# Gate layer in seven half products from chunk 2 on, 64x64-tile attention from pair 12, one new written order

## The chip, the cores and the metric

The kernel runs on one core of one Trainium2 chip. A core has TensorE (PE, matrix products into PSUM), VectorE (DVE), ScalarE (ACT), GpSimd (POOL) and SyncE (SP, which here only issues transfers). The metric is the device time of one execution in microseconds, as the median of several runs.

## What is computed

Attention over 8 batches x 8 heads, 576 positions of 64 numbers each, and then a gated feed-forward layer over the 4608 tokens of 512 numbers. The attention of a head is the sum of two parts:

```python
q_d = q.reshape(B, H, Sd, factor, D).mean(axis=3)     # factor 4, also k_d, v_d
out_d = sm_attn(q_d, k_d, v_d)                        # softmax attention at 144 positions
out_up = np.repeat(out_d, factor, axis=2)
mask = np.abs(pos[:, None] - pos[None, :]) < factor   # each position sees 7
scores = scale * np.matmul(q, k.transpose(0, 1, 3, 2))
scores = np.where(mask, scores, -1000000000.0)
...                                                   # softmax, out_local = attn @ v
return (out_up + out_local).astype(np.float32)
```

```python
gate = np.maximum(x @ w_gate, 0.0)     # x: 4608 x 512, w_gate: 512 x 1536
val = x @ w_val
return (gate * val @ w_out).astype(np.float32)        # w_out: 1536 x 512
```

## The kernel before

**Units of work.** Attention goes by 32 pairs of heads, four pairs to a batch. The feed-forward layer goes by nine chunks of 512 tokens. A chunk needs all pairs of the batches that its tokens lie in; chunk 7 needs the last pairs. Matrices are f16 on the chip, sums f32 in PSUM, which has eight banks of 512 f32 columns.

**A pair.** q and k come by POOL's transfers (`emit_load_q1`), are transposed by a transfer that SP issues (`emit_qkT`) and pooled 4:1 by VectorE (`emit_pool`). `emit_s1_mm` (line 421) makes the local scores in 12 matmuls of 64 rows, 128 columns of weights and 96 moving columns, which cover 96 queries with 112 keys used, and the pooled scores in four of 144 columns. ScalarE takes the exponentials (`emit_exp`, two halves, and the pooled ones), VectorE multiplies the band mask in (`emit_mask`, two halves). From pair 8 on `emit_s2w_mm` (line 577) makes numerators and denominators in one: the weights of a matmul are 64 columns of v beside 64 columns of ones, so that half of the 128 output rows are sums and half denominators; the two heads differ in which half is which. So logarithm (`emit_ln`), and division by multiplying (`emit_xnw`, line 609), go by head on 64 rows of 720 columns. `emit_xsum` adds the local and the repeated pooled part into xT, the layer's input. Pooled v is summed by POOL (`emit_v2`, `emit_v1`) from a transfer of its own. Pairs 4 to 7 use another form, `emit_den` and `emit_num` on 64-column tiles.

**The feed-forward layer.** `emit_h_mm` (line 635) makes 128 of the 1536 hidden columns for 512 tokens with four matmuls of 512 columns, for the gate and for the value weights. ScalarE takes the gate's relu into r1, VectorE multiplies it with the values in PSUM into gT (`emit_gate`). The output product of every chunk goes by `Unit` (line 694): two units of 256 tokens a chunk, each a 2x2 block product done with seven half products (p1 to p7) of six 256-column matmuls in place of eight, on sums and differences of the blocks (`sums`, VectorE). Partial results are copied to SBUF by ScalarE (`keep`) and added to others by VectorE (c11, c12, c22) or copied by ScalarE (c21).

`Block` (line 887) does the same for the gate layer: two hidden groups j and j+6 for 512 tokens, seven products of two 256-column matmuls each (`q`, line 910), three `keep` copies, three VectorE sums and one copy, then relu and multiplication in one VectorE instruction (line 950). It is used for ten blocks: chunk 7 from j = 2 and all of chunk 8.

**The order.** It is written out by hand: every engine runs its instructions as emitted. FRONT holds loads, pairs 0 to 7 and chunk 0; ORDER is a period of one chunk with four pairs, repeated by `emit_periods`; TAIL holds the rest of the output layer and chunks 7 and 8. A token such as `hg/0/0` names a step, its argument and its half of the chunk. FRONT's 14 wide warm-up matmuls on zeros come first on TensorE; POOL's first own work is the load of pair 0's k.

Of the kernel before, what the change touches and what calls it, by code (L numbers as in the profile page):

```python
# [73 lines left out]
TAIL = """  # L74
p/1/60 wg/2/ hv/0/70 keep/1/60 hg/0/70 gate/5 gate/4 hv/1/70 relu/0/70 sumhi/0/60 next/0 hg/1/70
sumhi/1/60 next/1 xs/0/7 hg/1/71 relu/1/70 xs/1/7 wg/0/ p/2/60 qg/1/72 gate/0/70 qg/2/72
keepg/1/72 hg/0/71 relu/1/71 tg/11/72 gate/1/70 p/6/60 sum/2/60 hv/0/71 keep/2/60 wg/1/
relu/0/71 hv/1/71 xs/2/7 gate/0/71 qg/1/73 qg/6/72 p/7/60 c11//60 keepg/2/72 xs/3/7 keepg/1/73
qg/7/72 wg/3/ hv/0/72 keepg/3/72 keep/3/60 qg/6/73 qg/5/72 qg/4/72 tg/22/72 p/4/60 gate/1/71
qg/3/72 c21//60 p/5/60 sum/0/61 tg/21/72 tg/12/72 qg/2/73 hv/1/72 keepg/2/73 tg/11/73 sum/1/61  # L80
qg/7/73 gateg/0/72 p/1/61 keepg/3/73 c22//60 qg/5/73 qg/4/73 gateg/1/72 qg/1/74 tg/21/73 hv/0/73
tg/22/73 keepg/1/74 xs/0/8 keep/1/61 qg/2/74 sum/3/60 qg/1/75 qg/6/74 tg/11/74 qg/3/73 p/6/61
tg/12/73 keepg/2/74 qg/5/74 p/3/60 keepg/1/75 qg/2/75 c12//60 qg/7/74 hv/1/73 gateg/0/73
keepg/3/74 tg/11/75 qg/4/74 p/2/61 tg/22/74 tg/21/74 gateg/1/73 qg/6/75 qg/1/80 qg/3/74
keepg/1/80 hv/0/74 tg/12/74 keep/2/61 xs/1/8 keepg/2/75 qg/5/75 c11//61 qg/2/80 sum/3/61 qg/7/75
hv/1/74 keepg/3/75 tg/22/75 qg/4/75 sum/2/61 p/5/61 gateg/0/74 qg/6/80 qg/3/75 gateg/1/74 p/7/61
tg/12/75 hv/0/75 xs/2/8 keepg/2/80 xs/3/8 tg/21/75 qg/2/81 gateg/0/75 qg/7/80 hv/1/75 keepg/3/80
tg/11/80 keep/3/61 qg/1/81 p/4/61 keepg/1/81 tg/11/81 qg/4/80 c21//61 qg/5/80 c22//61 hv/0/80
tg/21/80 tg/22/80 gateg/1/75 qg/1/82 qg/3/80 keepg/1/82 qg/5/81 tg/12/80 hv/1/80 sum/0/70 p/1/70
gateg/1/80 qg/6/81 gateg/0/80 p/3/61 keepg/2/81 sum/2/70 qg/7/81 hv/0/81 keepg/3/81 sum/1/70  # L90
keep/1/70 c12//61 qg/2/82 tg/22/81 qg/4/81 hv/1/81 tg/11/82 qg/3/81 qg/6/82 tg/12/81 p/2/70
sum/3/70 keepg/2/82 p/6/70 tg/21/81 gateg/0/81 qg/7/82 sum/0/71 keep/2/70 qg/5/82 qg/2/83
keepg/3/82 p/7/70 tg/22/82 qg/4/82 keep/3/70 qg/1/83 qg/3/82 keepg/1/83 p/4/70 tg/12/82
gateg/1/81 hv/0/82 c21//70 c11//70 qg/6/83 tg/11/83 p/5/70 keepg/2/83 sum/2/71 tg/21/82 p/1/71
gateg/0/82 qg/7/83 c22//70 keep/1/71 qg/1/84 qg/2/84 keepg/3/83 qg/5/83 hv/0/83 keepg/1/84
tg/22/83 qg/3/83 qg/6/84 tg/12/83 qg/4/83 p/3/70 tg/11/84 tg/21/83 gateg/0/83 keepg/2/84 hv/1/82
sum/1/71 qg/7/84 gateg/1/82 qg/1/85 keepg/3/84 p/6/71 keepg/1/85 c12//70 qg/5/84 part/20/80
qg/2/85 tg/22/84 hv/1/83 part/00/80 sum/3/71 qg/3/84 qg/4/84 tg/12/84 hv/0/84 tg/21/84
gateg/1/83 p/2/71 tg/11/85 qg/6/85 c11//71 hv/1/84 keepg/2/85 gateg/0/84 keep/2/71 qg/5/85
gateg/1/84 qg/7/85 p/5/71 keepg/3/85 p/7/71 part/00/81 tg/22/85 qg/4/85 part/20/81 keep/3/71  # L100
hv/0/85 part/01/80 part/01/81 part/21/81 p/4/71 part/10/80 part/30/80 c22//71 qg/3/85 c21//71
hv/1/85 tg/12/85 tg/21/85 gateg/0/85 p/3/71 gateg/1/85 p/1/81 part/22/81 c12//71 p/1/80
part/21/80 part/11/80 part/31/80 p/2/80 keep/1/80 part/02/80 part/12/80 keep/1/81 p/2/81 c11//80
part/10/81 p/6/80 part/22/80 part/11/81 part/30/81 p/5/80 part/32/80 keep/2/80 part/02/81
part/12/81 p/7/80 p/6/81 keep/3/80 c22//80 p/4/80 keep/2/81 part/31/81 c11//81 p/7/81 c21//80
part/32/81 p/5/81 keep/3/81 p/3/80 c22//81 p/3/81 c12//80 p/4/81 c12//81 c21//81
"""
LATE = ("gate/5/1", "gate/4/1", "next/0/1", "next/1/1")
ORDER = """
p/1/0 gate/5/1< scores/a/0 keep/1/0 gate/4/1< hg/0/0 exp/a0/0 sumhi/0/0 sumhi/1/0 exp/a1/0  # L110
hv/0/0 mask/a0/0 ed/a/0 mask/a1/0 p/2/0 next/0/1< relu/0/0 next/1/1< o/a00/0 o/a01/0 c11//0
o/a10/0 ln/a0/0 o/a11/0 sum/2/0 p/6/0 v/a/1 sum/3/0 p/5/0 keep/2/0 pool/b/0 v2/b/0 ln/a1/0 p/7/0
hg/2/0 keep/3/0 after/3/0 v1/a/1 inv/a/0 c22//0 p/4/0 gate/0/0 v2/a/0 p/3/0 xn/a1/0 c21//0 relu/2/0 hg/1/0
xn/a0/0 qk/a0/1 hv/2/0 relu/1/0 qk/a1/1 c12//0 xsum/a/0 scores/b/0 qk/a2/1 next/0/0 hv/1/0
exp/b0/0 v/b/0 exp/b1/0 hg/4/0 mask/b0/0 gate/1/0 v4/a/1 ed/b/0 hg/3/0 mask/b1/0 relu/4/0
gate/2/0 v1/b/0 o/b00/0 o/b01/0 o/b10/0 pool/a/0 ln/b0/0 o/b11/0 hv/4/0 v2/a/1 ln/b1/0 hv/3/0
gate/4/0 inv/b/0 v4/b/1 next/1/0 p/1/1 relu/3/0 xn/b1/0 v4/b/0 p/2/1 keep/1/1 qk/a3/1 hg/5/0
xn/b0/0 qk/b0/1 p/6/1 gate/3/0 relu/5/0 qk/b1/1 scores/a/1 next/2/0 keep/2/1 next/3/0 hg/0/1
# [50 lines left out]
def kernel(  # L169
# [23 lines left out]
    NJJ = D_FF // 128  # L193
    LEAD = 4
    NTP = 9
    NVP = 11
    VS = 7
    NK = NJJ // 2
    B0 = 1
# [947 lines left out]
```

## Time and profile before

| | |
|---|---|
| median of 3 runs | 345.66 us (345.18 to 346.06) |
| profiled execution, span from first to last instruction | 343.5 us |
| mean granted TensorE clock | 0.998 |
| TensorE busy, matmuls | 335.8 us, 3244 |
| VectorE, ScalarE, POOL busy | 295.2, 218.3, 181.9 us |
| line 638, gate and value matmuls of 512 columns | 352 and 432 |
| line 650, gate multiplication, mean of one | 680 ns |
| line 757, `keep` copy of 128x256, mean of one | 373 ns |

The span leaves out what lies around the instructions, so the median stands a little above it. A busy share on the page counts time in which at least one instruction of the engine is under way; matmuls overlap, so the mean duration of one (379 ns for 512 columns) is longer than its distance to the next. Idle time of an engine stands with the instruction ahead of which it falls, and with what ended it.

### The profile page before, as it was taken

What the parts mean: (1) busy time and instruction counts of PE and PEld (TensorE: products, weight loads), DVE (VectorE), ACT (ScalarE), POOL (GpSimd) and SP (SyncE); (2) the same over time, 40 slices, a digit from 0 to 9 for tenths busy, and PEclk for the clock granted to TensorE, in tenths of its full rate; (3) what the DMA queues carried; (4) which work ended last, traced back from release to release, by engine and by line L of the source; (5) the groups of instructions that cost most, each with busy time, mean ns of one, the idle gap of its engine ahead of it and who ended that gap; (6) DMA issues with size and microseconds to landing.
All of it is one profiled execution on the core that took longest, in us unless ns stands there. A gap on an engine that the chain in (4) does not pass through costs nothing.

```text
span 343.5 us, 8292 instructions
## 1 busy us (share of the span) xinstructions
PE 335.8 (98%) x3244; PEld 216.0 (63%) x3244; DVE 295.2 (86%) x546; ACT 218.3 (64%) x423; POOL 181.9 (53%) x232
## 2 busy tenths in 40 slices
PE   7899999999999999999999999999999999999996
PEld 3765556756575756575666656665766557768785
DVE  6695679988999999999999999999999798886892
ACT  3878766767767776676667767776677633334222
POOL 8986547776999893969297878740300000000000
PEclk9999999999999999999999999999999999999999
DMA  9999999999999999999989996991100001001023
GB/s 133 165 170 187 186 191 160 148 163 159 213 139 176 148 183 87 132 133 163 125 100 147 145 161 80 158 150 37 47 17 32 31 2 46 32 31 61 28 67 108
DMA packets 167882, 39.87 MB, mean 116 GB/s; under 512 B 149820, under 2 KB 164772, under 8 KB 167844
## 3 DMA queue, kind: packets, MB, share of 16 engines
q0 software_dynamic: 132160, 22.63, 92.1%
q1 hardware_dynamic: 35572, 16.71, 27.0%
q8 instruction: 25, 0.41, 0.5%
q14 instruction: 13, 0.11, 0.1%
q10 hardware_dynamic: 112, 0.02, 0.0%
HBM read 45.72 MB, written 9.44 MB: 161 GB/s over the span
## 4 chain that ended last, share of the span: by engine, by line
PE 90%; ACT 4%; DVE 3%; DMA 2%; issue 1%; POOL 0%; DVEq 0%; ACTq 0%; POOLq 0%
PE ps L638 48%; PE ps L723 23%; PE ps L910 4%; PE ps L584 4%; PE ps L437 2%; PE ps L426 2%; PE ps L592 2%; DMA vw<-in_v_dram 1%; PE ps L363 1%; PE ps L407 1%; DVE ee L453 1%; ACT qkT L377 1%; ACT ee L447 1%; ACT ed L461 1%; DVE xn L611 1%
## 5 line engine op out<-in xcount | busy, mean ns | idle before, releaser
L638 PE MATMUL ps<-xT,wv_sb 128*128 128x512 f16 x432 | 109.0, 379 | 0.0
L638 PE MATMUL ps<-xT,wg_sb 128*128 128x512 f16 x352 | 88.4, 380 | 0.0
L647 ACT ACTIVATE r<-ps 128x512 f16<-128x512 f32 x88 | 52.0, 596 | 31.6 <-PE ps L638 28.5
L638 PEld LDWEIGHTS <-wv_sb 128*128 128x128 f16 x432 | 40.4, 98 | 39.7
L650 DVE TENSOR_TENSOR gT<-r,ps 128x512 f16<-128x512 f16 x88 | 59.0, 680 | 6.7 <-PE ps L638 3.9
L638 PEld LDWEIGHTS <-wg_sb 128*128 128x128 f16 x352 | 32.6, 98 | 32.3 <-issue 0.2
L611 DVE TENSOR_TENSOR xn<-ps,rden 64x720 f16<-64x720 f32 x48 | 43.4, 905 | 5.3 <-ACT rden L607 4.1
L602 ACT ACTIVATE rden<-ps 64x720 f32<-64x720 f32 x48 | 36.7, 765 | 14.4 <-PE ps L592 13.3
L447 ACT ACTIVATE ee<-ps 112x576 f16<-112x576 f32 x64 | 38.8, 648 | 5.9 <-PE ps L437 4.9
L308 POOL DMA_DIRECT2D qk<-in_k_dram x46 | 33.9, 740 | 8.4 <-DMA qk<-in_q_dram 3.8
L308 POOL DMA_DIRECT2D qk<-in_q_dram x46 | 33.8, 740 | 6.9 <-DMA qk<-in_k_dram 1.7
L453 DVE TENSOR_TENSOR ee<-ee,cst_sb 112x576 f16<-112x576 f16 x64 | 32.3, 524 | 5.8 <-ACT ee L447 5.2
L723 PEld LDWEIGHTS <-gT 128*128 128x128 f16 x324 | 31.5, 98 | 9.0
L723 PEld LDWEIGHTS <-xo 128*128 128x128 f16 x288 | 27.4, 98 | 7.4
L333 POOL DMA_DIRECT2D vw<-in_v_dram x30 | 28.8, 960 | 5.8 <-PE ps L638 1.5
L350 DVE TENSOR_REDUCE qkd<-qkT 128x288 f16<-128x1152 f16 x23 | 30.9, 1344 | 0.0
L757 ACT COPY q<-ps 128x256 f32<-128x256 f32 x45 | 16.8, 373 | 21.1 <-PE ps L723 20.7
L723 PE MATMUL ps<-wo_sb,gT 128*128 128x256 f16 x216 | 28.0, 273 | 0.0
L723 PE MATMUL ps<-wt,xo 128*128 128x256 f16 x216 | 27.7, 272 | 0.0
L385 POOL TENSOR_TENSOR v<-v 72x512 f32<-72x512 f16 x21 | 24.8, 1182 | 3.7 <-DMA v<-in_v_dram 3.1
L920 ACT COPY vw<-ps 128x256 f32<-128x256 f32 x30 | 10.8, 374 | 20.7 <-PE ps L910 13.8
L570 DVE TENSOR_TENSOR xT<-xn 128x576 f16<-128x576 f16 x28 | 22.6, 808 | 0.5
(110 smaller groups left out, 556.9 us busy)
## 6 DMA issues: line engine op xcount, KB each, us to landing
out_dram<-y_sb SPq DMA_DIRECT2D x24, 256.0 KB, 4.0
vw<-in_v_dram POOLq DMA_DIRECT2D x30, 168.0 KB, 6.8
qk<-in_q_dram POOLq DMA_DIRECT2D x46, 72.0 KB, 6.6
qk<-in_k_dram POOLq DMA_DIRECT2D x46, 72.0 KB, 6.6
v<-in_v_dram POOLq DMA_DIRECT2D x21, 144.0 KB, 6.9
out_dram<-y_sb SPq DMA_DIRECT2D x22, 128.0 KB, 1.7
wg_sb<-in_moe_w_gate_dram POOLq DMA_DIRECT2D x4, 384.0 KB, 9.7
wv_sb<-in_moe_w_val_dram POOLq DMA_DIRECT2D x4, 384.0 KB, 10.5
```

What stands on the lines that cost most here:

```text
L308: nc.gpsimd.dma_start(dst.rearrange("p (j h d) -> p j h d", h=2, d=64)[:, :, hh, :], _dap(src, off + hh * S * D, [[D, 96], [NQ * D, NB], [ ...
L333: nc.gpsimd.dma_start(t, _dap(v, base, [[D, WK], [NQ * D, n], [1, D]]))
L350: nc.vector.tensor_reduce(out=qkd[hp % 2].rearrange("p i t -> p (i t)"), in_=qkT[hp % 4][:, 0 : 2 * S].rearrange("p (t f) -> p t f", f=4), ...
L385: nc.gpsimd.tensor_tensor(out=m, in0=t[:, :, 0:128], in1=t[:, :, 128:256], op=ALU.add)
L447: nc.scalar.activation(out=o, in_=ps[0:WK, p0 + 2 * g : p0 + 2 * g + 2, 0:288], func=AF.Exp, scale=scale)
L453: nc.vector.tensor_tensor(out=o, in0=o, in1=_sap(masks_sb, (0, WK), 96 * g, [[0, 2], [1, 288]]), op=ALU.mult,)
L602: nc.scalar.activation(out=rden[lo : lo + 64], in_=ps[de : de + 64, 4 + 2 * hh : 6 + 2 * hh, 0:360], func=AF.Ln)
L611: nc.vector.tensor_tensor(out=xn[lo : lo + 64], in0=ps[lo : lo + 64, 4 + 2 * hh : 6 + 2 * hh, 0:360], in1=rden[lo : lo + 64], op=ALU.mult,)
L638: nc.tensor.matmul(out=out, lhsT=w[:, kk, bass.ts(jj, 128)], rhs=xT[:, kk, c * TCH : (c + 1) * TCH], start=(kk == 0), stop=(kk == 3),)
L647: nc.scalar.activation(out=r1[j % 3], in_=h1, func=AF.Relu)
L650: nc.vector.tensor_tensor(out=gT[c % 2][:, jj, :], in0=r1[j % 3], in1=h2, op=ALU.mult)
L723: nc.tensor.matmul(out=out, lhsT=left[:, i, :], rhs=right[i], start=(first and i == 0), stop=(i == NK - 1), skip_group_check=True,)
```

## The change

**Gate layer.** From chunk 2's fourth block on, every gate block goes by seven half products: 39 blocks in place of ten. What remains in the old form are chunks 0 and 1 and three blocks of chunk 2, which have relu on ScalarE as before. The sums of the weights (`emit_ws`) lie in the second halves of the vw buffers and, one of them, over the masks.

**Partial sums in PSUM.** A new class `Seven` serves the gate blocks and, from chunk 1 on, the output units. Where `Block` and `Unit` copied a partial result to SBUF three times and added it three times, ScalarE now copies it to where the next product is accumulated in PSUM (after product 1 into d, after product 2 into b), and one other product (5) to SBUF; two results are copied out by ScalarE (11, 21), two summed by VectorE (12, 22). Relu and gate are one VectorE instruction.

**Attention from pair 12.** All matmuls use 64 rows and 64 columns of TensorE; four in turn are of four different quarters. Queries go in groups of 48 with 64 keys, head h on its own half of the output rows. Exponential, mask, logarithm and division are one instruction a pair on 128 partitions. Scores use banks 4 and 5, denominators 4 and 5 again, numerators 6 and 7. v is loaded in two parts of 64 rows, its pooled part as f32 by two SP transfers in place of one of POOL, and the pooled result is copied to the other half of the partitions by two SP transfers (`emit_dup`). Three POOL memsets clear the v4 buffers at the start.

**Order.** ORDER and TAIL are replaced by one list, MAIN, that names pairs, chunks and blocks outright. FRONT is as before; MAIN begins with the scores of pair 12.

```diff
+MAIN = """
+s1/12 hg/2/0/0 hv/2/0/0 relu/2/0/0 ws/2/1 exp/12 lq/18/2 hg/2/1/0 flip/15 gate/5/1@1 hv/2/0/1 v2/14 gate/4/1@1
+pool/13 sum/1/0/0/5/6 gate/2/0/0 p/1/0/1 lq/20/2 lq/18/1 ed/12 relu/2/1/0 hg/2/0/1 hv/2/1/0 sum/1/0/2/0/6
...
+e/8/0/12 s/8/1/5 y/8/0/1/1 e/8/1/22 y/8/0/0/0 e/8/1/11 y/8/0/0/1 y/8/1/1/1 y/8/1/0/0 p/8/1/4 e/8/1/12 e/8/0/21
+y/8/1/0/1 y/8/0/1/0 e/8/1/21 y/8/1/1/0
+"""
...
+    ZP = 12
...
-    v4 = ring(NV4, [72, 4, 256], FP16, "v4_")
+    v4 = ring(NV4, [128, 3, 256], FP32, "v4_")
...
+    for t in v4:
+        nc.gpsimd.memset(t, 0.0)
...
+    def emit_load_v4z(hp, h):
+        b, off = head_off(hp)
+        nc.sync.dma_start(
+            v4[hp % NV4][64 * h : 64 * h + 48],
+            _dap(v, off + h * S * D, [[4 * D, 48], [192 * D, 3], [1, 4 * D]]),
+        )
...
+    def emit_dup(hp, n):
+        o = vdz[hp % 3]
+        nc.sync.dma_start(o[64 - 64 * n : 112 - 64 * n, 1], o[64 * n : 64 * n + 48, 0])
...
+    def emit_s1z(hp):
+        r4, f = hp % 4, qkdflat[hp % 2]
+        for c in range(3):
+            for g in range(2):
+                for h in range(2):
+                    rows, lo = slice(64 * h, 64 * h + 64), 288 + 72 * c
+                    nc.tensor.matmul(
+                        out=ps[64 * g : 64 * g + 64, 4 + h, lo : lo + 72].rearrange("p (j t) -> p j t", t=12),
+                        lhsT=f[rows, SD + 48 * c : SD + 48 * c + 64],
...
+        t = qkT[r4]
+        for j in range(6):
+            for par in range(2):
+                for h in range(2):
+                    rows, lo = slice(64 * h, 64 * h + 64), 96 * j + 48 * par
+                    nc.tensor.matmul(
+                        out=ps[64 * par : 64 * par + 64, 4 + h, 48 * j : 48 * j + 48],
+                        lhsT=t[rows, S + lo - 3 : S + lo + 61],
+                        rhs=t[rows, lo : lo + 48],
...
+    def emit_denz(hp):
+        for par in range(2):
+            rows = slice(64 * par, 64 * par + 64)
+            for h in range(2):
+                nc.tensor.matmul(
+                    out=ps[64 * h : 64 * h + 64, 4 + par, 0:288],
+                    lhsT=ones_sb[rows, 0:64],
+                    rhs=eefull[hp % 2][rows, h, 0:288],
...
+        emit_downz(hp, 4, lambda rows, other, c: ones_sb[rows, 64:128])
+
+    def emit_numz(hp):
+        t, d = vz[hp % NL], vdz[hp % 3]
+        for j in range(6):
+            for par in range(2):
+                rows = slice(64 * par, 64 * par + 64)
+                for h in range(2):
+                    nc.tensor.matmul(
+                        out=ps[64 * h : 64 * h + 64, 6 + par, 48 * j : 48 * j + 48],
+                        lhsT=t[rows, 6 * h + j, :],
+                        rhs=eefull[hp % 2][rows, h, 48 * j : 48 * j + 48],
...
+        emit_downz(hp, 6, lambda rows, other, c: d[rows, other, c, :])
...
-    class Block:
...
+    class Seven:
...
+        def product(self, i):
+            out = (self.a, self.d, self.b, self.a, self.e, self.a, self.a)[i - 1]
+            n = len(self.left[i])
+            for t in range(n):
+                nc.tensor.matmul(
+                    out=out,
+                    lhsT=self.left[i][t],
+                    rhs=self.right[i][t],
+                    start=(i == 1 and t == 0),
+                    stop=(t == n - 1),
+                    skip_group_check=True,
+                )
...
+        def copy(self, i):
+            o, a = {1: (self.d, self.a), 2: (self.b, self.a), 5: (self.m, self.e)}[i]
+            nc.scalar.copy(out=o, in_=a)
+
+        def finish(self, i):
+            o = self.outs[i]
+            if i in (12, 22):
+                nc.vector.tensor_tensor(out=o, in0=self.b if i == 12 else self.a, in1=self.m, op=ALU.add)
+            else:
+                nc.scalar.copy(out=o, in_=self.d if i == 11 else self.a)
```

In a token of MAIN, `q/c/j/i` is product i of a gate block, `k` its copies, `o` its results; `p`, `s` and `e` are the same for an output unit; `hv` and `gate` are as before; `s1`, `exp`, `ed`, `mask`, `den`, `ln`, `inv`, `num`, `xn`, `xsum` are a pair's steps; `flip` is the transpose, `y` the store. `emit_downz` makes the pooled part of denominators and numerators in 12 matmuls of 48 rows and 72 columns.

## The prediction

> **What bounds the kernel now.** I read the page's first two parts and its chain first, to see which engine is full and where.
>
> ```profile
> span 343.5 us, 8292 instructions
> ...
> PE 335.8 (98%) x3244; PEld 216.0 (63%) x3244; DVE 295.2 (86%) x546; ACT 218.3 (64%) x423; POOL 181.9 (53%) x232
> ...
> PE   7899999999999999999999999999999999999996
> ...
> DVE  6695679988999999999999999999999798886892
> ...
> PE 90%; ACT 4%; DVE 3%; DMA 2%; issue 1%; POOL 0%; DVEq 0%; ACTq 0%; POOLq 0%
> ```
>
> TensorE is full from the third slice to the last but one, and the chain runs on it for 90% of the span. So a stage is worth what its matmuls take, as long as nothing else gets fuller. VectorE is close: nine tenths or more from slice 11 to 31. The view of engine time by stretches says how close (columns: window, its length, then busy time and instructions of each engine):
>
> ```profile
> 95.00:130.00 35.00, 35.00 (x324) 21.84 (x323) 32.85 (x53) 24.72 (x44) 32.84 (x43) 1.00 1.91 161
> ...
> 270.00:305.00 35.00, 35.00 (x241) 23.40 (x240) 29.63 (x61) 14.38 (x38) 0.00 (x0) 1.00 0.08 26
> ```
>
> In the middle TensorE works 35.00 of 35 us, VectorE 32.85, ScalarE 24.72. The second window already has gate blocks in seven half products, and TensorE is full there too; but ScalarE has 20 us to spare in it, and in the middle only 10.
>
> Matmul durations overlap, so costs are taken from one start to the next. The timeline of TensorE (start, length, line, shape, count):
>
> ```profile
> 148.78 0.82 PE L723 MATMUL ps<-wt,xo 128*128 128x256 f16 x6
> 149.53 0.25 PE L426 MATMUL ps<-qkd 64*72 64x144 f16 x2
> ...
> 149.81 0.29 PE L437 MATMUL ps<-qkT 64*128 64x96 f16 x6
> 150.03 1.04 PE L638 MATMUL ps<-xT,wg_sb 128*128 128x512 f16 x4
> 150.91 1.03 PE L638 MATMUL ps<-xT,wv_sb 128*128 128x512 f16 x4
> 151.77 0.82 PE L723 MATMUL ps<-wt,xo 128*128 128x256 f16 x6
> 152.42 0.29 PE L584 MATMUL ps<-ee,vw 112*128 112x96 f16 x3
> 152.55 0.23 PE L592 MATMUL ps<-ed,vd 72*128 72x72 f16 x2
> 152.62 0.29 PE L584 MATMUL ps<-ee,vw 112*128 112x96 f16 x3
> ```
>
> A 512-column matmul takes 0.216 us (151.77 - 150.91 over four), a 256-column one 0.109 (0.65 over six). Six 64-row matmuls of 96 columns pass in 0.13, 43 ns for two: two row tiles run at once. Entering the scores costs 0.096 (0.75 for six matmuls that need 0.65), leaving them as much: the price of each change of tile shape.
>
> **The gate layer.** 29 blocks change form (chunk 2 from its fourth, chunks 3 to 6, two of chunk 7). Each loses 8 matmuls of 512 columns, 1.73 us, and gets 14 of 256, 1.53 us (eight of line 910 take 0.87 in the chain). 29 x 0.20 = **-5.9 us**, all on the path.
>
> **Attention, pairs 12 to 31.** Before, a pair takes 0.60 us of TensorE for scores (149.53 to 150.03 and the change ahead of it) and 4 x 0.197 = 0.79 for lines 584 and 592 (five take 152.62 - 152.42), 1.39 in all, with two changes of shape. After, it has 88 smaller matmuls: scores 12 of 72 columns and 24 of 48, denominators 4 of 288 and 12 of 72, numerators 24 of 48 and 12 of 72, all on 64x64 tiles, written four tiles in turn. The nearest rows are the column tiles of the early pairs:
>
> ```profile
> 39.12 0.29 PE L527 MATMUL ps<-ee,ones_sb 112*64 112x288 f16 x2
> 39.24 0.23 PE L536 MATMUL ps<-ed,ones_sb 72*64 72x72 f16 x4
> 39.31 0.29 PE L548 MATMUL ps<-ee,vw 112*64 112x96 f16 x6
> 39.44 0.23 PE L557 MATMUL ps<-ed,vd 72*64 72x72 f16 x4
> ```
>
> Two of 288 columns take 0.12, two of 72 about 0.033, two of 96 again 0.043. So row tiles pair and column tiles pair; that four run at once no row shows. I take that they do: a group of four costs what two cost here, 0.033 for 72 columns, 0.122 for 288, and for 48 columns 0.028, between 0.022 (in proportion to 72) and 0.030 (a 65-column matmul of line 486, the smallest in the trace). Then scores and numerators are 3 x 0.033 + 6 x 0.028 = 0.27 each, denominators 0.122 + 3 x 0.033 = 0.22: 0.76 a pair. To that come 25 ns at each block's first group (as between the first matmuls at 149.53 and 149.62) and the changes of shape: the new order has 41 such blocks for 20 pairs, 82 changes x 0.096 = 7.9 us. In all 15.2 + 1.0 + 7.9 = 24.1 us against 27.8: **-3.7 us**. If only two tiles run at once, the 15.2 become about 30.1: +11.3 in place of -3.7.
>
> The Trainium skill speaks against the small matmuls: "TensorE: Matmul & The Clock Gate", on the 56 ns gap, says that starts are never less than some 25 ns apart however few the columns. Read for each instruction, 88 x 25 ns would make a pair 2.6 us and the span some 25 us longer. In this trace two of line 548 take 43 ns, so the rule cannot hold across tiles; read for each tile, it would put 25 in the place of my 28.
>
> **The start.** New are three POOL memsets of 128x768 f32, which stand on POOL's queue ahead of its first load, and TensorE's first real work, weight loads (PEld) included, waits for that load:
>
> ```profile
> 1.30 1.05 POOL L303 DMA_DIRECT2D qk<-in_k_dram  x1 [0.85 <-POOLq L1131]
> ...
> 5.90 0.67 PEld L363 LDWEIGHTS <-qk 96*64 96x64 f16 x24 [0.42 <-DMA qk<-in_k_dram]
> ```
>
> The nearest row, 112x768 f16 on POOL (line 1066), takes 819 ns; by elements three are 2.5 us, by bytes 4.9. POOL issues its loads one behind the other from here (1.30, 2.33, 3.27), so the later ones shift too, and nothing covers it: **+2.5 us** (0 to 4.9).
>
> **VectorE and ScalarE.** Whole-kernel sums hardly move. VectorE loses 20 masks (524 ns, -10.5), trades 40 divisions of 64x720 for 20 of 128x720 (905 and 906, -18.1), loses 16 output sums (-6.7) and gets 48 gate sums (421, +20.2), 20 input differences (419, +8.4) and smaller weight sums (+0.5): -6.2 us. ScalarE trades 58 relus (596), 20 exps (648) and half the logs for 171 copies of 128x256 (373): -1.4. Of these copies 110 go from PSUM to PSUM, which no row shows; at 0.27 (373 less the overlap) to twice 373 ns each, ScalarE stays under 80% of the span, so I take 373 and nothing on the path.
>
> What counts is when. Taking the new written order from where pair 12's scores stand (95 us in the profile), and counting each VectorE instruction at its duration less the 0.08 us that back-to-back ones overlap: beside the first 40.1 us of matmuls stand 78 VectorE instructions, 40.5 us (46.7 without overlap); beside 70.0 stand 67.8; beside 100.2, 94.7; later less. In the window 95 to 130 this count gives 31.4 where 32.85 are busy, 1.046 times. So the first stretch needs 42.4 us against 40.1: **+2.3 us** (0 to 8, where no overlap is left over the first 70 us), and from there TensorE leads again.
>
> **Queues.** SP gets 40 halves of v as f32 and 40 small copies from SBUF to SBUF; POOL loses 20 v4 loads (745) and gets 20 more v loads. A DMA transpose behind a late store on SP would hold a pair's scores, and SP's waits for y_sb reach 13.4 us; but the order writes each transpose two to three pairs (some 20 us) ahead of its scores, against 7.8 us to landing. Without that cover a pair would wait up to 13 us; with it, 0. The loads left after 95 us are the same pairs', in about the same time. The last stores end the kernel as before: 0, with 1 us each way.
>
> **The sum.** Against the profiled execution: 343.5 - 5.9 - 3.7 + 2.5 + 2.3 = 338.7 us of span. The median of the runs, 345.66, is 2.2 above that span, so the forecast is **340.9 us**, 1.4% faster.
>
> **Rivals.** (1) *Tiles run two at a time*, in the scores, denominators and numerators of the 20 pairs: +15.0 on the sum, 356 us, slower. It decides from 0.24 us a pair on (4.8 us over 20 pairs): a group of four 48-column matmuls at 40 ns in place of 28, the others in proportion. For it: no trace row with four; against it: both pairings are complete. 16%. (2) *VectorE or ScalarE paces the middle*: the seeded sums make each block a chain of product, copy, product on two banks, and TensorE waits where the copy stands behind other work. At +8 for the stretch in place of 2.3, 347 us; some 345 to 352. For it: 90% of VectorE's window is already needed; against it: TensorE is full beside such blocks at 270 to 305. 22%. (3) *The covers hold*: no stall in the first stretch and part of the memsets beside waits at 6 to 22 us: 336 to 338. 12%. My forecast, 338.5 to 344.6, has 50%.
>
> About 0.3% is what a measurement of this kernel can tell from no change (344.6 to 346.7). The forecast's 50% and the third rival's 12% are faster: 62%. Of the second, 8 are within 0.3% and 14 slower; with the first, 30% are slower. The range 336 to 353 leaves out the first rival but for its mild end, and little at the bottom.
>
> **What would show it.** Right: TensorE's first f16 flip near 8.4 us; groups of four starting within some 12 ns and 28 ns apart; 0.218 for each pair of gate matmuls with the next behind it; TensorE idle of 2 to 3 us between 95 and 145 us, released by VectorE, and none later. Wrong: 48-column groups at 40 ns or more; flips still at 5.9; idle before the products released by ScalarE's copies all along chunks 3 to 6; or a pair's scores waiting for a transpose.

## The result, and the profile after

After the change the kernel takes **357.21 us** (355.80 to 358.99, four runs), against 345.85 us (345.18 to 346.06) for the kernel before, run beside it: a ratio of 1.0346, 95% interval 1.0307 to 1.0385. The prediction was 340.9 us, 336 to 353, so it has the wrong sign, and the time lies above the range. Medians and ranges in this document count every run, while the ratios, and they alone, leave out the runs that lie over 1.5% above their kernel's fastest (two of e11's four; the one profiled of e15).

The page of the kernel after, the same parts that were shown of before:

```profile
span 355.2 us, 10891 instructions
...
PE 333.4 (94%) x4458; PEld 229.1 (65%) x4458; DVE 292.9 (82%) x552; ACT 210.6 (59%) x496; POOL 176.2 (50%) x230
...
PE   7899999989997897999999999999989999999994
...
DVE  5595679998999899899998999999878876676572
...
PEclk9999999999999999899999999999999999999998
...
PE 41%; DVE 3%; ACT 2%; issue 1%; DVEq 0%
```

TensorE is busy for less time than before (333.4 us for 335.8), and the span is 11.7 us longer. Its row has holes in the second quarter of the span, where it was full, and the clock row a slice of 8. VectorE has 2.3 us less to do over the whole (6.2 were forecast).

The view of engine time by stretches (columns: window, length, then busy time and instructions of PE, PEld, DVE, ACT, POOL; granted clock, DMA share, GB/s):

```profile
95.00:130.00 35.00, 31.56 (x490) 20.20 (x489) 33.11 (x54) 19.95 (x41) 30.60 (x39) 1.00 2.19 148
130.00:165.00 35.00, 31.49 (x526) 22.20 (x527) 31.85 (x55) 20.79 (x53) 19.47 (x27) 0.95 1.85 151
165.00:200.00 35.00, 32.41 (x530) 22.54 (x518) 32.99 (x56) 21.15 (x52) 29.02 (x40) 1.00 1.91 180
...
270.00:305.00 35.00, 35.00 (x377) 25.63 (x376) 26.64 (x55) 18.34 (x54) 0.00 (x0) 1.00 0.08 28
```

From 95 to 200 us TensorE lacks 2.6 to 3.5 us in every window, with VectorE at 31.9 to 33.1 of 35. From 270 us on, where no pair's data is loaded any more (DMA share 0.08), TensorE is full.

Where the time came from, between the two profiled executions. I count as a wait every gap between two matmuls that is 0.15 us longer than the first one's columns need at the granted clock.

| | before | after | difference | predicted |
|---|---|---|---|---|
| last matmul's end | 340.3 us | 350.4 us | +10.1 | |
| of it: waits up to 60 us | 6.2 | 7.1 | +0.9 | +2.5 |
| waits from 60 to 310 us | 0.8 | 16.4 | +15.6 | +2.3 |
| half-speed clock (3.41 us) | 0 | 1.7 | +1.7 | 0 |
| the rest: matmuls and small gaps | | | -8.1 | -9.6 |
| from the last matmul to the end | 3.2 | 4.8 | +1.6 | 0 |

The matmuls gave nearly what they were to give. The waits took twice that. Of the 16.4 us VectorE released 10.3, ScalarE 1.6, and 4.5 have no semaphore at all. The longest of these, in the timeline of TensorE:

```profile
138.27 0.28 PE L751 MATMUL ps<-qkT 64*64 64x48 f16 x13
140.87 0.28 PE L751 MATMUL ps<-qkT 64*64 64x48 f16 x11 [2.31 <-issue]
141.08 0.39 PE L1105 MATMUL ps<-xT,vw 128*128 128x256 f16 x2
141.31 1.14 PE L1105 MATMUL ps<-wo_sb,gT 128*128 128x256 f16 x6
142.25 1.49 PE L1105 MATMUL ps<-wt,xo 128*128 128x256 f16 x6
```

TensorE stops in the middle of one pair's local scores, after 13 of 24 matmuls, for 2.31 us, with nothing to wait for; "issue" says only that. The queue that brings instructions has 35 packets of 16 KB in place of 25 (its row below). That is one for some 256 instructions of TensorE, if matmuls and weight loads are counted (8916 over 35, before 6488 over 25). One of them was under way from 137.66 for 1.83 us. That a late packet is what TensorE stood for is inferred from these times. The duration of a packet alone does not decide it: of ten that took 1.36 us or more between 60 and 310 us, three were followed by such a stop and seven by none, and before, eight of 1.3 to 1.7 us were followed by none. Behind the stop six 256-column matmuls take 0.94 us and then 1.42 for 0.65: the clock was granted at half speed from 141.66 on for 3.41 us.

From the view of transfers, before and then after (the last number is the median from issue to landing):

```profile
q8 instruction: 25, 0.41, 0.5%
...
qkT<-qk SPq DMA_TRANSPOSE x23, 7.8
```

```profile
q8 instruction: 35, 0.57, 0.7%
...
vd<-vd SPq DMA_DIRECT2D x40, 18.0 KB, 5.9
qkT<-qk SPq DMA_TRANSPOSE x23, 8.4
```

And SP's queue from 95 us on has a wait that it never had, for POOL's sums of pooled v, ahead of the small copies (engine and line, released by, us in total, times, longest):

```profile
SPq L513 <- POOL vd L509: 25.9, 10, 5.7
...
SPq L434 <- POOL v L500: 9.6, 6, 3.0
```

Transposes, loads and output stores stand behind these waits on the same queue; before, none of the waits listed for SP in this stretch was for POOL.

### The profile page after: what moved, and what is told of

Its sections match the earlier page's. It is cut to its first block, busy times and chain, and to the rows that moved or that the text cites. A ratio compares the mean times of both kernels' runs of the same rounds, so it can differ in the third digit from the quotient of the medians.

```text
span 355.2 us, 10891 instructions
## 1 busy us (share of the span) xinstructions
PE 333.4 (94%) x4458; PEld 229.1 (65%) x4458; DVE 292.9 (82%) x552; ACT 210.6 (59%) x496; POOL 176.2 (50%) x230
## 2 busy tenths in 40 slices
DMA packets 171990, 44.30 MB, mean 125 GB/s; under 512 B 154812, under 2 KB 167844, under 8 KB 171940
## 5 line engine op out<-in xcount | busy, mean ns | idle before, releaser
L1116 ACT COPY ps<-ps 128x256 f32<-128x256 f32 x110 | 39.4, 366 | 43.0 <-PE ps L1105 41.0
L1222 DVE SCALAR_TENSOR_TENSOR gT<-r,ps 128x512 f16<-128x512 f16 x63 | 42.2, 679 | 8.6 <-PE ps L863 7.9
L1105 PE MATMUL ps<-xT,vw 128*128 128x256 f16 x270 | 47.2, 273 | 0.4 <-ACT q L1116 0.4
L1105 PE MATMUL ps<-xT,wg_sb 128*128 128x256 f16 x234 | 42.7, 274 | 1.1 <-DVE xT L1121 0.7
L1105 PEld LDWEIGHTS <-vw 128*128 128x128 f16 x270 | 25.8, 98 | 8.6 <-issue 0.7
L1123 ACT CAST r<-ps 128x256 f16<-128x256 f32 x58 | 21.1, 377 | 17.0 <-PE ps L1105 11.4
L1121 DVE TENSOR_TENSOR r<-ps,q 128x256 f16<-128x256 f32 x58 | 23.7, 417 | 8.4 <-PE ps L1105 3.9
L863 PE MATMUL ps<-xT,wg_sb 128*128 128x512 f16 x120 | 30.4, 380 | 0.0
L1105 PEld LDWEIGHTS <-wg_sb 128*128 128x128 f16 x234 | 22.2, 98 | 10.0 <-issue 1.7
L699 DVE TENSOR_TENSOR xn<-ps,rden 128x720 f16<-128x720 f32 x24 | 21.6, 902 | 5.2 <-PE ps L777 1.9
L500 POOL TENSOR_TENSOR v<-v 128x384 f32<-128x384 f32 x20 | 23.2, 1159 | 2.6 <-DMA v<-in_v_dram 2.2
```

Source lines behind the costliest of these rows:

```text
L500: nc.gpsimd.tensor_tensor(out=v2full[hp % 2][:, 0:3, :], in0=t[:, :, 0:128], in1=t[:, :, 128:256], op=ALU.add)
L699: nc.vector.tensor_tensor(out=xn, in0=ps[:, num : num + 2, 0:360], in1=rden, op=ALU.mult)
L863: nc.tensor.matmul(out=out, lhsT=w[:, kk, bass.ts(jj, 128)], rhs=xT[:, kk, c * TCH : (c + 1) * TCH], start=(kk == 0), stop=(kk == 3),)
L1105: nc.tensor.matmul(out=out, lhsT=self.left[i][t], rhs=self.right[i][t], start=(i == 1 and t == 0), stop=(t == n - 1), skip_group_check=True,)
L1116: nc.scalar.copy(out=o, in_=a)
L1121: nc.vector.tensor_tensor(out=o, in0=self.b if i == 12 else self.a, in1=self.m, op=ALU.add)
```

## The experiments

Five theories, each named in the expectations. **C**: POOL's sums stretch VectorE's instructions with two inputs in SBUF. **S**: the seeded partial sums make chains through ScalarE. **F**, later split into **I** (TensorE's instruction blocks come late because the DMA engines are full) and **D** (a pair's own transfers, the small copies above all, come late). **Q**: it is the transposes' place on SP's queue. The waits are those of the profiled execution from 60 to 310 us; in the last column stands the granted clock of that execution.

The runs of one kernel spread over 1 to 8 us, so a difference of 2 us between two rows is not clear of that.

| kernel | us, median (range) | ratio to before (95%) | waits: all, VectorE, none | clock |
|---|---|---|---|---|
| after | 357.21 (355.80-358.99) | 1.0346 (1.0307-1.0385) | 16.4, 10.3, 4.5 | 0.993 |
| e1 POOL's sums on one column | 355.26 (355.00-357.43) | 1.0268 (1.0226-1.0311) | 14.8, 6.6, 6.8 | 0.993 |
| e2 no late loads | 347.92 (346.61-350.60) | 1.0056 (1.0026-1.0085) | 8.2, 6.5, 0.5 | 0.995 |
| e3 gate layer in full products | 364.53 (363.63-364.89) | 1.0518 (1.0483-1.0553) | 18.2, 8.8, 3.2 | 0.997 |
| e4 POOL's sums paced | 355.30 (353.44-357.82) | 1.0280 (1.0226-1.0334) | 13.9, 11.4, 0.5 | 0.993 |
| e5 no small copies | 352.27 (349.63-354.14) | 1.0169 (1.0115-1.0222) | 15.0, 11.5, 1.1 | 1.0 |
| e6 no late f32 loads of v | 352.93 (352.73-356.90) | 1.0220 (1.0163-1.0278) | 14.6, 11.0, 1.6 | 0.998 |
| e7 no late loads of q and k | 350.92 (349.02-353.03) | 1.0139 (1.0082-1.0196) | 11.6, 9.7, 0 | 0.999 |
| e8 before, no late loads | 345.63 (344.46-351.05) | 0.9983 (0.9960-1.0006) | 3.0, 3.0, 0 | 1.0 |
| e9 six groups in one matmul | 352.16 (348.51-353.58) | 1.0168 (1.0098-1.0239) | 17.4, 13.6, 0 | 1.0 |
| e10 e2 and e1 | 347.02 (344.49-348.66) | 1.0021 (0.9987-1.0055) | 5.8, 3.3, 0.9 | 1.0 |
| e11 memsets later | 356.94 (351.47-359.64) | not given | 16.0, 8.8, 2.9 | 0.995 |
| e12 e11, copies by POOL | 349.92 (348.15-351.51) | 1.0118 (1.0065-1.0172) | 10.0, 8.3, 0 | 0.995 |
| e13 transposes early | 364.71 (362.89-366.45) | 1.0524 (1.0465-1.0583) | 22.6, 11.8, 1.7 | 0.981 |
| e14 e12, transposes early | 354.70 (352.36-356.00) | 1.0226 (1.0175-1.0277) | 14.4, 5.7, 0 | 0.988 |
| e15 e14, sums paced | 355.32 (351.37-357.05) | 1.0216 (1.0154-1.0277) | 14.6, 6.6, 0 | 0.986 |
| e16 e12, three loads later | 351.46 (349.78-355.04) | 1.0136 (1.0084-1.0187) | 11.6, 8.5, 0.7 | 0.995 |
| e17 e16, sums paced | 352.36 (350.94-355.49) | 1.0176 (1.0129-1.0223) | 12.8, 10.1, 0 | 0.995 |

**e1: POOL's sums on one column** (the pooled part is left out).

```diff
-in0=t[:, :, 0:128], in1=t[:, :, 128:256]       # emit_v2, o likewise; emit_v1z the same
+in0=t[:, :, 0:1], in1=t[:, :, 128:129]
```

> The changed kernel with POOL's two sums of each pair from 12 on (pooled v, lines 500 and 509) cut to one column of 64 or 128; the pooled part of the output is left out by that. Order, transfers and every other instruction stay. Theory C (collision): in the changed kernel VectorE's sums of two SBUF inputs stand still while POOL sums, 16.1 us in all by the trace against 6.3 before, and VectorE sets the pace between 95 and 235 us; then the stretched VectorE instructions go to under 2 us in all and the time falls by 8 to 12 us, to 345 to 349. Theory F (TensorE waits for its own instructions and for the small copies of pooled v): 356 to 357. Theory S (the chains of seeded partial sums through ScalarE hold TensorE): 356 to 357.

The collision itself is plain. In the kernel after VectorE's sums of 128x768 beside POOL's sum (first VectorE, then POOL):

```profile
183.56 0.55 DVE L942 TENSOR_TENSOR xo<-gT,xo 128x768 f16<-128x768 f16 x1
...
184.63 1.90 DVE L942 TENSOR_TENSOR xo<-gT 128x768 f16<-128x768 f16 x1
```

```profile
185.09 1.01 POOL L500 TENSOR_TENSOR v<-v 128x384 f32<-128x384 f32 x1
```

0.55 us alone, 1.90 with POOL's sum inside it. Over the kernel 23 VectorE instructions are stretched by 16.1 us in all (before: 14, 6.3 us), and in e1 one, 0.7 us. The Trainium skill has this in "SBUF — State Buffer", on who interferes with whom: a VectorE instruction with two inputs in SBUF and a GpSimd one that reads SBUF lock each other out for a whole instruction, whichever starts first holding the other up. The rows agree that VectorE's instruction stands still; but here it started 0.46 us ahead of POOL's sum and was the one held up, by 1.35 us, while the sum took 1.01. The time fell by 2 us only, in ranges that overlap: C by itself is a small part.

**e2: no loads of q, k and v from pair 19 on** (later pairs work on what lies in the buffers).

```diff
-lq/p/i lv/p/i l4/p/h          # tokens of MAIN with p of 19 and more
```

> The changed kernel without the transfers of q, k and v from pair 19 on (pairs 19 to 31 compute on what lies in the buffers); all instructions of TensorE, VectorE and ScalarE stay, and POOL's sums. Theory F: the fetches of TensorE's instructions take 1.2 to 1.8 us in the middle, beside busy DMA engines, against 0.9 at the start; without the traffic they take 0.9 to 1.0, waits of TensorE with no semaphore go from some 4.5 us to under 2, those for the small copies go, and the time falls by 4 to 7 us, to 350 to 353. Theory C: POOL's sums still run beside VectorE's, at other places: 354 to 358. Theory S: 356 to 358.

9.3 us less than the kernel after, more than F expected. Its stretches:

```profile
95.00:130.00 35.00, 33.12 (x503) 20.81 (x500) 34.38 (x56) 21.22 (x43) 24.02 (x32) 1.00 1.71 143
130.00:165.00 35.00, 34.47 (x568) 24.10 (x567) 33.65 (x61) 23.79 (x58) 6.58 (x8) 1.00 0.35 81
165.00:200.00 35.00, 34.85 (x640) 24.84 (x639) 32.49 (x62) 22.68 (x56) 6.49 (x9) 1.00 0.33 76
```

With the DMA share at 0.35 TensorE is almost full, with the same matmuls in the same order, and VectorE gets through more instructions in each window than in the kernel after (56, 61 and 62 for 54, 55 and 56). From 130 to 200 us the waits that VectorE releases fall from 4.0 to 1.2 us, so most of those were not VectorE's own work being too long. Over the whole stretch 6.5 of 10.3 us stay.

**e3: the gate layer undone**, full products in the new order.

```diff
-q/c/j/1 ... q/c/j/7 k/... o/... ws/... xs/...
+hg/c/j/0 relu/c/j/0 hg/c/j/1 relu/c/j/1
```

> The changed kernel with the gate layer of chunks 2 to 8 undone: full products of 512 columns and a relu on ScalarE, in the places of the new order; sums of inputs and weights gone. The 64x64-tile attention, the output layer and POOL stay. TensorE gets 39 blocks x 0.20 = 7.8 us more, VectorE loses 78 sums of 0.34, 28 differences of 0.34 and the weight sums: some 40 us. Theories C and S (VectorE, or the seeded chains, hold TensorE): the 14 us of stalls mostly go and the time is 349 to 355. Theory F: the stalls of TensorE stay and 7.8 us come on top: 360 to 365.

7.3 us slower, and as many waits (18.2 us), although VectorE has only 25 to 29 us of work in 35 here. S falls for the gate layer: the waits do not come with its chains. The output units keep their seeded sums in this run, so S is not tested for them; ScalarE releases 6.2 us of the waits here and 1.6 in the kernel after. The gate term itself was nearly right: 7.3 us for 39 blocks x 0.20 = 7.8.

**e4: POOL's sums paced**, each held until VectorE does something that reads PSUM or has one input (all of the reference is computed).

```diff
-... v2/19 ...
+... holdsum_2_0_1_0_5 v2/19 ...    # POOL first copies a column of that step's result
```

> The changed kernel with POOL's sums of pairs 14 to 31 moved in POOL's order, by some tokens, to stand beside VectorE's steps that read PSUM or only one SBUF input (pooling, division, gate), each held back by a one-column copy on POOL that reads what VectorE wrote just before that step. The same work otherwise. Theory C: stretched VectorE instructions fall from 16 us to 3 to 8, and the time by 4 to 10 us, to 347 to 353. Theories F and S: 356 to 360, as POOL only gets more waits.

2 us, as e1, and again in ranges that overlap. By a count like that above 18 VectorE instructions are still stretched here, by 10.2 us in all, where 3 to 8 were expected, so this run tests C only in part. With e1, which takes nearly all of the stretch away, C comes out small as long as the other delays stand.

**e5, e6, e7: whose traffic?**

```diff
-dup/p/n                        # e5, all pairs
-l4/p/h                         # e6, p of 19 and more
-lq/p/i                         # e7, p of 19 and more
```

> The kernel after without the 40 small SBUF-to-SBUF copies of pooled v (the other half of the buffer holds a constant from the start, so a part of the pooled attention is left out). e2 showed that late DMA traffic costs 9 us; this asks whose. Theory D (the pair's own small transfers): the copies land after 5.9 us, POOL's sums and the numerators wait for them, and without them the time falls by 3 us or more, to 352 or less. Theory I (TensorE's instruction blocks come late because the DMA engines are full): the copies move 0.7 MB of 44.3, the time stays at 354 to 357 and the waits of TensorE with no semaphore stay at 4 to 7 us.

> The kernel after without the f32 loads of v for the pooled part from pair 19 on (26 transfers of 144 KB on SP; POOL sums what lies there). Theory I-SP (the new SP transfers, twice the bytes of the old ones, fill the DMA engines): the time falls by at least half of what e2 gained, to 352 or less, and the waits with no semaphore fall below 3 us. If instead all loads together fill the engines, this third of the late bytes gains 2 to 3 us only: 353 to 354.5.

> The kernel after without the q and k loads from pair 19 on (52 transfers of 72 KB on POOL; the transposes go on with what lies there). Theory I-POOL (the many small packets of POOL's queue, which takes 91% of the DMA engines' time, hold the instruction blocks up): the time falls by 5 us or more, to 351 or less. Theory I-SP: it falls by 1 to 3 us, to 353 or 355.

4.9, 4.3 and 6.3 us less. The loads of e6 and e7 together give 10.6, where e2, which also leaves out the 26 other loads of v, gave 9.3; with ranges some 4 us wide that neither adds up nor fails to. The copies of e5 are not among e2's loads. In all three the waits with no semaphore fall to 1.6 us or less and the half-speed clock is gone from the profiled execution. D nearly gets what it asked for from e5 (352.27 for 352), but I-SP and I-POOL, which were rivals, both come out at or near their numbers; the three do not tell one guilty transfer.

**e8: the control**, the kernel before without its late loads.

```diff
-lambda hp, a: f(hp + 4, *map(int, a)) if hp + 4 < NP else None
+lambda hp, a: f(hp + 4, *map(int, a)) if hp + 4 < 19 else None
```

> Control: the kernel before without the loads of q, k and v from pair 19 on. Theory I (the smaller matmuls need 35 instruction blocks in place of 25, and in dense stretches): the kernel before loses nothing to late traffic, and the time stays at 345 to 346.5. If late traffic slows every kernel alike, it falls by 5 us or more, to 341 or less, and e2's gain says nothing of the change.

No change that can be measured. The loads were there before, with a DMA share of 1.91 from 95 to 130 us, and cost nothing. The change made the kernel sensitive to late traffic, of which it also has more: 44.30 MB in all for 39.87.

**e9: fewer instructions of TensorE**, the same transfers.

```diff
-        for j in range(6):     # 48 columns each, in emit_s1z and emit_numz
+        # one matmul of 288 columns a quarter
```

> The kernel after with one matmul of 288 columns per quarter in place of six of 48, in the local scores and the numerators (so five of six groups meet another group's keys or values, which leaves that part of the computation out). A pair has 48 matmuls in place of 88, the data transfers are the same. By the costs of one group (0.122 us for four of 288 against 6 x 0.032) TensorE saves 0.07 us a block, 2.8 us over 20 pairs. Theory I (instruction blocks come late): the blocks fall from 35 to about 29, the waits with no semaphore from 4.9 us to 1 or less, and with the clock drop behind one of them the time falls by 7 us or more, to 350 or less. Theory D (the pair's own transfers come late) : only the 2.8 us, 354 to 355, with the other stalls as they are.

28 instruction packets for 35, no wait without a semaphore, clock 1.0: that part of I is shown. Yet the time falls by 5 us, not 7, and the waits in all do not fall: 17.4 us for 16.4, VectorE's 13.6 for 10.3. What is left over for the matmuls is 3.2 us less, near the 2.8 of the size alone; the rest is the clock. What TensorE no longer waits for its instructions it waits for VectorE, which is at its limit there:

```profile
95.00:130.00 35.00, 30.50 (x345) 18.58 (x343) 34.51 (x53) 19.05 (x40) 32.42 (x43) 1.00 2.09 162
130.00:165.00 35.00, 33.57 (x408) 23.10 (x406) 33.87 (x61) 23.93 (x59) 24.43 (x34) 1.00 1.85 174
```

**e10: e2 and e1 together.**

> e2 (no q, k and v loads from pair 19 on) and e1 (POOL's sums on one column) together; e2 still had 8.2 us of stalls, most of them released by VectorE. Theory C (VectorE instructions stretched beside POOL's sums make these): the time falls from 347.9 to 344 or less. Rival: the written order itself leaves VectorE too much in the first stretch, as the count of the prediction had it; then it stays at 346.5 to 348, with stalls of 7 us or more.

In the profiled execution the waits fall to 5.8 us and the span to 343.2. The median falls only by 0.9, within the ranges, and the other runs were granted a lower clock (0.987 to 0.999; the quickest, 344.5, has 0.999). The time is in the rival's range, the waits are below its 7 us; e10 does not decide.

**e11: the memsets behind the loads of pairs 3, 4 and 5.**

```diff
-    for t in v4:
-        nc.gpsimd.memset(t, 0.0)
+loadv/3 clear/0 ... loadv/4 clear/1 ... loadv/5 clear/2      # FRONT
```

> The kernel after with the three POOL memsets of the v buffers behind pairs 3, 4 and 5's loads in place of ahead of the first load. Term +2.5 us of the prediction: the time falls to 354 to 355.5. The trace after has the first load issued 1.5 us later than before but pair 12's scores only 1.2 us later, most of it from another stall: then the time falls by 0.5 us or not at all, 356 to 358.

0.3 us less in the median, in runs that lie 8 us apart: nothing that shows. The waits up to 60 us go from 7.1 to 6.5.

**e12: e11, and the small copies by POOL** (all of the reference is computed).

```diff
-        nc.sync.dma_start(o[64 - 64 * n : 112 - 64 * n, 1], o[64 * n : 64 * n + 48, 0])
+        nc.gpsimd.tensor_copy(out=o[64 - 64 * n : 112 - 64 * n, 1], in_=o[64 * n : 64 * n + 48, 0])
```

> e11, and pooled v copied to the other half of the partitions by two POOL copies of 48x192 in place of two SP transfers. All of the reference is computed. e5 says that the 40 small transfers cost 5 us. Theory D and I both: the time falls to 351 to 353. If POOL's 40 added copies stretch VectorE's instructions as its sums do (theory C), it stays at 354 or more.

7.3 us less than the kernel after, the best whole version of the change, still 1.2% slower than before. So the copies' way over SP cost more than their 0.7 MB of 44.3 would suggest: e5, without them and with the memsets in place, gave 4.9 us, and e12's 7.3 contain the memsets' move as well, for which e11's runs are too far apart to give a share. One large wait is left, on VectorE, ahead of a 2.44 us gap of TensorE:

```profile
153.56 0.41 DVE L1120 TENSOR_TENSOR xT<-ps,q 128x256 f16<-128x256 f32 x1
156.87 1.35 DVE L463 TENSOR_REDUCE qkd<-qkT 128x288 f16<-128x1152 f16 x1 [2.89 <-DMA qkT<-qk]
158.13 0.45 DVE L763 TENSOR_TENSOR ee<-ee,near_sb 128x576 f16<-128x576 f16 x1
158.50 0.42 DVE L1120 TENSOR_TENSOR r<-ps,q 128x256 f16<-128x256 f32 x1
158.84 1.28 DVE L1221 SCALAR_TENSOR_TENSOR gT<-r,ps 128x512 f16<-128x512 f16 x2
```

The pooling waits for a transpose; mask, sum and two gate multiplications that other steps need stand behind it on VectorE. The edit of e16 below looks for its cause at pair 18's transpose, but by the written order it is pair 20's: pair 18's pooling ran at 142.97 us without a wait. SP's queue ahead of pair 20's transpose:

```profile
144.98 5.91 SPq L432 DMA_DIRECT2D v<-in_v_dram  x3
151.11 4.02 SPq L456 DMA_TRANSPOSE qkT<-qk  x2
```

```profile
SPq L432 <- POOL v L498: 15.1, 2, 10.6
```

Two of SP's waits for POOL's sums end between 140 and 152 us, 15.1 us in all, ahead of the f32 loads of pairs 22 and 24; the longer one, 10.6 us, holds the whole queue until 144.98. Pair 20's transpose stands behind these loads, is issued at 151.11 and lands at 156.84. So at this place theory Q's chain stands in the trace, from POOL's sum over SP's queue to VectorE and to TensorE's gap.

**e13: the transposes early**, each right behind its q and k loads.

```diff
-... l4/20/0 ... p/2/0/1 v1/18 flip/18 dup/18/1 ...
+... s1/14 ... flip/18 ... l4/21/1 ... l4/20/0 ... dup/18/1 ...
```

> The kernel after with each DMA transpose of pairs 15 to 31 written earlier on SP's queue, right behind its q and k loads, ahead of the f32 loads of v and the small copies that it stood behind (up to 160 steps of the written order). Theory Q (SP's queue: transposes stand behind transfers that wait for POOL, and VectorE's pooling, with masks and gates behind it, waits for them): the time falls by 3 us or more, to 354 or less. Rival, theory I (what counts is the traffic in all, and its own instruction blocks are what TensorE waits for): it stays at 355.5 to 358.5, with the wait with no semaphore near 138 us as before.

7.5 us **slower**: Q's remedy fails as it stood. On TensorE:

```profile
133.57 0.20 PE L771 MATMUL ps<-ed,vd 48*64 48x72 f16 x1
140.02 0.27 PE L771 MATMUL ps<-ed,vd 48*64 48x72 f16 x1 [6.25 <-DMA vd<-vd]
```

The early transposes wait on SP for their loads (22.2 us for k), and now TensorE waits 6.25 us for a small copy behind them.

**e14, e15: the same on e12; e16, e17: only three f32 loads moved behind pair 18's transpose.** e15 and e17 add e4's holds.

```diff
-... l4/21/1 ... l4/21/0 ... l4/20/0 ... v1/18 flip/18 ...     # e16
+... v1/18 flip/18 l4/20/0 l4/21/1 l4/21/0 ...
```

> e12 (pooled v copied by POOL, late memset) with the early transposes of e13. e12 has left one wait of 2.6 us near 157 us in which VectorE waits 2.9 us for a transpose, and a half-speed clock for 3.4 us after it. Theory Q: both go, the time falls by 3 to 4.5 us to 345.5 to 347, about the time of the kernel before. Otherwise another wait takes its place, 348.5 to 350.5.

> e14 with POOL's sums held until VectorE steps that read PSUM or have one input, as in e4. If the stretched VectorE instructions still cost anything once the transfers are out of the way (as e10 against e2, 1 us), the time falls 1 to 2 us below e14's; if the holds delay the sums past their numerators, it rises.

> e12 with three f32 loads of v (pairs 20 and 21) written behind pair 18's transpose on SP in place of ahead of it; everything else as in e12. e13 and e14 showed that a transpose moved far ahead holds copies and output stores back; here it only passes loads that wait for POOL and are wanted much later. If SP's order is what e12's wait of 2.6 us near 157 us comes from, that wait and the half-speed clock behind it go and the time falls by 2 to 4 us, to 346 to 348. If the transposes' late q and k loads are, it stays at 349 to 351.

> e16 with POOL's sums held as in e4. By e10 against e2 the stretched VectorE instructions are worth about 1 us once TensorE waits for little else: 0 to 2 us below e16. If the holds make POOL's loads later, and with them SP's transposes, 1 to 5 us above it.

At 354.70 and 355.32 us e14 and e15 lie above all that was expected of e14, and e16 (351.46) and e17 (352.36) are no faster than e12. In e14 the wait at 157 us is gone, and an output store is late in its place:

```profile
141.86 0.75 DVE L811 TENSOR_TENSOR xT<-xn 128x576 f16<-128x576 f16 x1
150.37 0.42 DVE L1114 TENSOR_TENSOR y_sb<-ps,q 128x256 f32<-128x256 f32 x1 [7.75 <-DMA out_dram<-y_sb]
```

VectorE waits 7.75 us for an output buffer. SP had stood 9.0 us on a q load for a transpose, up to 140.0 us; the store went out behind it at 143.0 and took 7.3 us to land (median 3.1 in the kernel after). e16 did not move the wait, but it was aimed at the wrong transpose: the loads that it moved stood ahead of pair 18's, while pair 20's is issued at 150.20 there, still behind the loads of pairs 22 and 24 (issued over 8.68 us, with 12.9 us of waits for POOL's sums), and VectorE waits 4.38 us for it. What those loads cost is thus untested. e17 is no better than e16, nor e15 than e14: no run shows a gain by the holds here.

## Why the prediction was wrong

**The matmuls: right, a little too high.** -8.1 for -9.6. The gate term is 7.3 us over 39 blocks in e3, 0.19 a block for 0.20. Four tiles do run at once, as assumed, and rival 1 falls: that its 356 us is next to the result is chance. (By its own sum it would have decided from 37 ns a group on, not 40: 4.8 of 15.0 us is a third of 28 ns.)

```profile
97.06 0.29 PE L739 MATMUL ps<-qkd 64*64 64x72 f16 x12
97.18 0.36 PE L751 MATMUL ps<-qkT 64*64 64x48 f16 x24
97.47 1.04 PE L863 MATMUL ps<-xT,wg_sb 128*128 128x512 f16 x4
```

A pair's scores take 0.41 us to the next product, where two tiles at a time, twice as many groups at the distances below, would need over 0.6. Within a group the starts are 3 to 4 ns apart, and the next group follows after 32 ns (28 predicted) for 48 columns, 35 (33) for 72.

**The start: too high.** The three memsets take 2.09 us together and the first load is issued at 2.77 for 1.30, but the weight load that waits for it starts at 6.28, where 8.4 was the sign of being right and 5.90 that of being wrong. The waits up to 60 us grow by 0.9 for 2.5, and e11 does not show even that in the time.

**VectorE in the first stretch: right there, missed behind it.** +2.3 (0 to 8) was counted on durations from before, "and from there TensorE leads again". VectorE releases 3.4 us of waits from 95 to 145 us, near the forecast, and 5.7 later, where none was expected. Without late loads it still releases 6.5 us in all (e2), and 3.3 where POOL does not stretch it either (e10). The step that failed in it is "counting each VectorE instruction at its duration": the new order has no step that keeps POOL's sums off VectorE's, as the old one had (`after`, a POOL copy that waits for the unit's last VectorE sum), and the stretch grew from 6.3 to 16.1 us.

**The queues: this is the step that failed most.** The prediction put them at 0: "the order writes each transpose two to three pairs (some 20 us) ahead of its scores, against 7.8 us to landing", and "The loads left after 95 us are the same pairs', in about the same time". Taking the late loads away gives 9.3 of the 16.3 us that were missed, with no effect on the kernel before (e8); taking the small copies off SP gives 4.9 (e5), and with the memsets moved 7.3 (e12).

How the traffic costs this is shown only in part. The cover in the written order is there, but a transfer is issued only when SP gets to it, and the prediction counted the 40 copies but not what they wait for and what stands behind each: SP stands 25.9 us for POOL's sums ahead of them. That total is no measure of the loss, though. It is larger in faster runs (48.6 us ahead of the copies in e2, 53.5 ahead of the f32 loads in e12) and smaller in the slowest (14.9 ahead of the copies in e13); what counts is which step is late for it, as at 157 us in e12. Nor did the prediction count TensorE's own instruction packets, ten more, on DMA engines that were already busy for 90% or more up to 222 us by the page's row, and at times closer together: 4.9 us apart at the least (187.64 and 192.50 us), where before no two from 95 us on were less than 10. The waits beside them are 4.5 us.

The half-speed clock, worth 1.7 us each time, was not in the sum at all. In the profiled execution (0.993 granted) one such stretch lies ahead of the last matmul; another, 0.9 us by the same reckoning, lies behind it, where nothing is lost. By the lowest grant of the four runs, 0.987, the loss would be up to some 3.7 us, an estimate (0.013 of 357 us, less 0.9).

**Rival 2** (347 us, 345 to 352) had the engine right: VectorE releases 10.3 of the 16.4 us of waits, and 6.5 of the 8.2 that are left in e2. Its mechanism, that TensorE waits for the copies of seeded sums, is not what the kernel after shows (ScalarE releases 1.6 us), and its range ends below the result.

What the runs show is a kernel with two engines near full that wait for each other in order: TensorE at 31 to 34 and VectorE at 32 to 34 of 35 us. A transpose, a small copy or a store that came 3 to 8 us late stopped VectorE or TensorE, and then the other (e12, e13, e14), and taking one such delay away brought out another (e9, e13, e14). Before, TensorE alone was full, VectorE had 2 us of 35 to spare, none of SP's waits listed for this stretch was for POOL, and the late loads cost nothing.

**Left open**: how the 9.3 us divide between instruction blocks and the pairs' transfers, since every run that eased one eased the other or let VectorE take its place; what an order gains in which no load that waits for POOL's sums stands ahead of a transpose; and the 1.6 us more behind the last matmul, which no run took apart. The old attention form in the new order was not tried: its scores need four PSUM banks that the new order uses for other things.

## What to carry to other kernels

Before costing a transfer at zero because it is written early enough, follow its queue: ask of each transfer ahead of it what that one waits for, and who else stands behind. When a change relieves the full engine, look at who is nearly full too (here VectorE, with 32.85 of 35 us) and at what was hidden only because the first was full: every cover has to be priced anew. Many small matmuls are cheap by the columns, but here they brought ten more packets of instructions, over the same DMA engines as the data. And before moving a transfer, make sure by the written order which pair's it is.

## What the runs showed of the hardware

**Instruction blocks.** In the kernel after TensorE stopped three times, 0.6 to 2.3 us, with no semaphore beside a packet of its instruction queue that took 1.4 to 1.8 us; the next matmul came 3.0 to 3.2 us after the packet's start. With 28 packets for 35 (e9), or without the late loads (e2), these waits are 0 and 0.5 us in all. How long a packet takes does not follow the traffic alone: up to 70 us seven took 0.89 to 0.99 beside a DMA share of 1.9, and in e2 one of 3.09 us (at 68.4) stopped nothing. The Trainium skill, "Runtime: NRT & Kernel Launch", on instruction fetch mechanics, calls the crossing of such a block mostly hidden. In the kernel before there is no such wait; in this one they come to 4.5 us in the profiled execution.

**The clock.** Gaps of 1.9 to 3.4 us in TensorE's work (after, e1, e4, e12, e16, e17) were followed by one stretch of 3.41 us at half speed, and gaps of 4.9 to 6.3 us (e13, e14, e15) went with one of 6.83. The length of a gap does not decide it: 2.68 us in e11 (up to 140.12) and 2.32 in e1 (up to 113.14) were followed by none, while one of 1.47 in e11 (up to 169.55) was.

**POOL across partitions.** A POOL copy of 48x192 between partitions 0 to 47 and 64 to 111 takes 0.34 us (median of 40 in e12, the longest 0.97), in place of a transfer that took 5.9 us to land (median, kernel after).
